# Spacing the weight loads of a two-layer recurrent transformer kernel in its plan, and moving the zeros of its value tiles

## The chip, the cores and the metric

The kernel runs on one core of a Trainium2 chip. The core has five engines that work side by side and wait for each other through semaphores: the PE (TensorE, matrix products), ScalarE (ACT in the profile), VectorE (DVE), GpSimd (POOL) and SyncE (SP, which here only starts transfers). GpSimd starts transfers too. The metric is the device time of one execution in microseconds (us).

## The reference

Two layers are applied twice, with the same weights each time. Layer A is an attention that goes through the sequence in 64 segments of 32 rows; eight memory rows are put in front of each segment, and the memory of the next segment is the output of this one. So the segments follow each other strictly. Layer B is a gated feed-forward. The reference, cut:

```python
def A(x, mem0, Wq, Wk, Wv, Wo, seg_len):          # x: 1 x 2048 x 512, 32 heads of 128, memory 8 rows
    mem, outs = mem0, []
    for s in range(n_seg):                        # 64 segments
        h = concatenate([mem, xs], axis=1)        # 8 + 32 rows
        q, k, v = h @ Wq, h @ Wk, h @ Wv          # per head
        p = softmax(where(mask, q @ k.T * scale, -1e9))
        o = (p @ v) @ Wo
        mem = o[:, :M, :]                         # goes on into the next segment
        outs.append(o[:, M:, :])
    return concatenate(outs, axis=1)

def B(x, w_gate, w_up, w_down):                   # 512 -> 1792 -> 512
    return (sigmoid(x @ w_gate) * (x @ w_up)) @ w_down

x = x + A(layernorm(x));  x = x + B(layernorm(x))
x = x + A(layernorm(x));  x = x + B(layernorm(x))
```

## The kernel before

The kernel runs the two passes of layer A interleaved: step t does segment t of the first pass and segment t - 6 of the second, so most matmuls have 80 columns (twice 40 rows). The attention weights stay in memory on the core. The feed-forward weights do not: each block of 128 rows loads all of them again, in pieces of 256 KB, into rings of three tiles each for `wg`, `wu` and `wd`.

The program is not written down in its final order. Each operation is added to a planner as a task, with the engines that may do it, an assumed duration in ns, what it reads and writes, and for a transfer the bytes `nb` and a latency `lat`. The planner then walks through time with a simple picture of the chip, and takes on each free engine the ready task that comes first in a stored sequence. The order in which the tasks start in this picture is the order in which the instructions stand in the program, engine by engine. So the assumed numbers change no instruction's real duration; they change which instruction stands where, and what a load waits for.

```python
class Planner:
    LAT = {"PE": 205.0, "DVE": 110.0, "ACT": 128.0, "POOL": 40.0, "SP": 4000.0}
    BUS, LEAD, TAIL, BIG, ROOM, POOL0 = 345.0, 2000.0, 1900.0, 200000, 300.0, 2000.0
    ...
    def forward(self):
        ...
        # GpSimd does not take a big load while the transfer queue is too far ahead
        if e == "POOL" and T[q[1]].nb >= self.BIG and bus > now + self.LEAD + self.ROOM:
            aside.append(q)
            heapq.heappush(events, (bus - self.LEAD - self.ROOM, 1, 0))
            continue
        ...
        if tk.nb:                                  # when a transfer lands in the plan
            bus = max(bus, now + self.LEAD) + tk.nb / self.BUS
            done = bus + self.TAIL
```

A feed-forward weight load, and the matmuls that need it (`B` is called `ffn`):

```python
pl.add("POOL", 760, lambda wg=wg, fs=fs: nc.gpsimd.dma_start(out=wg[:], in_=self.wgv[:, :, fs]),
       r=[("wo", self.H - 1)], w=[gk] + bt, lat=4600.0, nb=2 * self.DC * P * P * 2)      # 262144 bytes
...                                                # the same for wu and wd
GB = pl.buf(self.bank, "bg")                       # PSUM bank; at most 3 of kind "bg", 3 of kind "v"
pl.add("PE", 2 * DC * mm_ns(n), mm, r=[xk, gk, uk], w=[GB])        # L1034: gate and up
...
pl.add("PE", 2 * mm_ns(512), dm, r=[hk, dk], w=[DB])               # L1058: down
```

The spacing in the plan is carried over to the chip: each big load gets a wait on the last PE task that had ended, in the plan, when the load started.

```python
for tk in order:
    if tk.on == "POOL" and tk.nb >= self.pl.BIG:
        k = bisect.bisect_right(ends, tk.start + 1.0)
        if k:
            pace[tk.idx] = pes[k - 1].idx
...
    if tk.idx in pace:
        self.tc.add_manual_dep(nc.cur_bb.bb.instructions[-1], seen[pace[tk.idx]], self.SYNC, ...)
```

GpSimd also clears tiles at the start, among them rows 32 to 63 of the three value tiles, which must be zero because the product with the probabilities runs over 104 rows and only 80 of them hold values:

```python
for k, t_ in enumerate(self.vsb):                  # 3 tiles, [128, 2, 1024] bf16
    pl.add("POOL", 1860, lambda t_=t_: nc.gpsimd.memset(t_[32:64], 0.0), w=[...])
```

Other lines that the profile names: L834 query and key products, L848 scores, L862 to L879 softmax, L891 transposes of the probabilities, L914 product with the values, L932 product with Wo, L682 and L759 value products (in full tiles and in strips of 32 rows), L651 and L1002 transposes, L641 the power of the layer norm, L1150 matmuls on a zeroed tile `hot` that only keep the PE busy, L1158 copies on ScalarE, L1160 copies on VectorE.

Of the kernel before, what the change touches and what calls it, by code (L numbers as in the profile page):

```python
# [20 lines left out]
P = 128  # L21
MEM = 8
SEG = 32
L = MEM + SEG
# [29 lines left out]
;AiJ8O<e#G00LqO81Dpg?#XRnVk#=3t=h#IvY(+`&AcaUnw28X=}w4PEU`lamQ$OIpo&~BNLA*v)8_<LH_4?mqJB9BPoKci*ww~Xp)w?&I~Z~HBw)uo$QQx-;`OBtJB6xFkfX<JRX)Vp<pwi9-$>Wq  # L54
_|(bG)+LpP5u9QR&=8D1Ynn6`50CKLwAk)5&^1p?M5ud)kVw93aBRaf&q*h3JD;4Ll!hLLRQPlXLpBL((>{FtthZ7-6|on*(`sH;)5N{G{S1Q90H4$Ds(Z|lR0?u{tEC`hGou%Gd$027BUNC18E{L7
&F)C#zgM=c{I#A@-&_cC)EA7@W+gT`4MdX5Z<e~;XBiD0b6uuRW+zpR5($+!E$PDMb#05@4J<$Tgbufr7=j;14{hrW2XG!0l#o*PC@hFM#?tGT6r9A)HO<OTl13v9w~w#YRv#=MeGw>(WPyyKB1!Cc
Kh4|7Igw&V<X;!vy&=LHaWFD+p%tHofD6TKnCr|$0|AFqvW@S36%&P<g+xP2B_-vSh>c$a21QjVdvj4tl9}JapL&LM5}J5*o7wnh^Q!>iVtS2`P40J?4<hBBT!d|vv(!65R|43k?j2ySJjDalB!M5q
0+48MexK=31cV1eCa9G4=FYg0$8pi>H?<rNeHU|4WBR@wD1Gs|PFGshWAv`I7x-d~N80)*!h<rk^pgB$#xYA8^3<cts1d0#zHflM9<Kn7(59`#h`o$$C3RD8h@e)twdz3~B2ztI-Zl=|>k0(jtN&EZ
M+6(<F}aBH*s>|C;8a&rtX~-hVfXD<h6X~?EY^Zz6gi0r<U9i(>VzMAJE*Se^dOX0rgm~|E!=Xx9r_TrDzwc0+!EsrL~)Soi;Oi;HUFoX=*13GNv&ZMt+nOX`)*VNh$X0KjWg3pTl4!=JTaVM>8>HL
847pxUL$IK>({v}PsAcpnD@J-@IuLIgQ_IF-p$l|+Y>W~r)<#N&!w#H{kF|?*-F)dKD!wIm9RA>Xq1LJ2Wok$$C~rlfyiSKy6@0|B)T>H1NJUFd;RLgL9*+RWXJx?QqOd)T>|2m?ALU71CBZm<cDwJ  # L60
ofeVYFF39i25%~7b6dl-Szt!`b-re7-B~{crk)vUJfH3kryVB*(7RtNQcI^zOIYp)7{`a^=;Ws?VKJ)*;5|5eFn<A8j@jc(VHL0+6_~v%wV&XqjHFI1AMwQBZ_@YmyTCt@Qzj;730DaCS=SbvOAy#R
b*Sqhur|1y$EZAJ1;bN)$+7$=8C~Lo*;Hrsm6OARmhEF(!s4()P-}CtMCgoM?F;6)-20FEkTpVQ?bo7ItMHTYNO09xJ8>TRYqO*|GTUQCd45=t;TTVkp2mNk?%z5;D%B{z#Ebw;WE>3bKD}~M8i*5L
$e=1i%D_S#Xj_x8+IE7dP}suAIjN}(q`q-QX}`+C;;ka@YIYS}2&7Qm<f>$oR=*)*I`|4m=LBs&(Q!LT1;Q>IcRD}S@&NS($)uVXEtMjw&vna78_S7Mlec%u<sO~)mngVW7>T6h$iUEYqnP|puo0fT
r`TMWmfzTh<G(BWf)#O<t!5y74sH_M&Z=4btV4*QNiV4<6V&W{e4I*MRws<_x%O(Y$MOrVEeoVyG3@QId`iX^5p6WM8c$3kg{SO5{l)C7p}yI}4CaD%!l71<san+GQCJk+p}VL~bP8uJkGY0kBT5vj
R1-ykT=4ub<1V=InVbNwl6!S8td%+Mz~(^8*x_;GPz>g2$XSqPPbev-o^hs!?7@QMWhY0y`$$F&9ixb+y?zfPat4Fi!9lU1Pg8vI&j;+LEM7n1u5gq)5A1Ko>q-PF|9fW{quMQz<qKqqK}c6+c+Fjd
F2Og)Y9!)bPmT?k!nyf?G)Xd5=K!N;M>3lVNE}6P7cnNl4OcV-lb#H=@=tK=cxvWNb6Kzv_sM|QR*voi!Zn`=jVh#r4%=)b)LoY?p68N_b^*GwHypnifULn;3GbuLC`r8UsPf=vI`9TA8B`u7X6;#N
!m;8u{taW8B=ZYuhxB9*O)W#qWE!7AhkB;}qi!mEvlh~K9<WKouf7f7L{WqYu}gBY?M2l)tmM{7Nu9QfNYq2fype%X^IJqHYC#4qRVe@~VAmgkHN0m|{HV|^C7s-nFqYkrf5W*?th9LSf%-sleh6@c
h^ng>)=Ywn0;fa0nILORo|102uL^+jVT+d!dfe14p)J)dlR1OmXGPfL-y36CdZ?|rcwsM+BZtm`w8J3fxRJ_+4s6&Uno5Bi_*n7}#H?RWtb4Zi&|Rm*Zz2TNh&lO#7UGXjAdPbxNHJ|g_4H9xi8*?+
MVBMu<!Xv~TZTq;8n*wB%JxEkrMB;<8}+JQA_z}uHS0xv7nP9H@k*%6*aeBVs5=pHO`T#wtNbE}<|rvhkGwM4E;)G7MYl*s$M|Wb`VP#Re6BgJ2e|qxS57L9bw0omcy&;%c|qJ{(zEm8exBk>6kxD6
nxVA2ia}k;GP?4Q>rk`340>lGd_YNLHVqb}3U`2d_S9|fmyu5SUIT|O7ON>xv0wK}^_@-tG>TrZhfljsqoh53@*TnfA+x8TWApG@0BvWO*~un;YD}WAVB`%Ocf`pScOENCOw%nLPstoRq_M;BvJb5(  # L70
9>G{3K!TD={~^49yc*?mqNgGc5Y9`P58_BH7xzKfFPZ`Ggp&M|jB=z<d!Mk7Cu<-nf0j1JK3){GSBO4_Z3Mk$J5xc&swnx5Kk-kQoc7)9dxA>^2fUiVDTTmJUDH?8OUBger)cDkijH?|-1he<?wF<H
Kk8n|8|izgJ<_+Vk)Z%3oi>GZ`YrtS_<S>K*lk;jOpIxLM&`FEhlm;kTVot3q|rBV<2zngWEolEcY`CX0@8r^=@owQoZaOwbLKKB5WYQ9ATLkYUM6T<RE#Alz-kX8EZD3nbuenjKH^OPbNyU7wVF39
J|$N?ZCflXfOCh2K(_Em93YBI;A{RAe?$e%i<!x3qM)(DsREc-Dh@|;RaZz{Ll-kv@m+)8ts@E#1fh>1JG<CwJGMH~u9ZKP6{u*%L%13ENMvluV`@wIuxV8YVb)3nInI0dgPfb`)M|>%G*b`M+Eyyj
jqV1HH2csu+-gLZN!CnTWAkDUlaM(`w_&JSZYO|vzbuZQ*3PLKI)0ga%QxJf?^bvE1F+>TX${_k_>1jSMGlLjj>YIweuT`hQ?^&irkU=_GGO$DDI{>cW;6n|9j!RtGy%M~@}&-R?w${HkEp`&f?|dq
hRtUsFPVbG8-up0*v|ZA*EkVFY50Mj6?9y)4JpMkyC%&ExAc7!4gc+R=<99a<n4o-&ZXVwa+QJY{b7j7VJQE>0Y8piWd%VS48RwJid2BAY66-+%Wl?{`zc4poCF9pm`~fP$UOlA=c$<fqq-V>@sE|3
N2~z048Fb9GPveh@ym=U;`2r6)y6OIo@9rAM5%*f0;`aD^F_98-YHoGz4`oih2?qv)`GZ>QO83Z7HvL5ku>dZiIYj=NO}ck>~z#R9*jNmjj|h>R>*3!dO|Qd*G>CP;It>Jo_T;GC~pf_h0K-$@9NV(
Yc?%zR57pmwZF@3z4b@VylrfJgY8hUsQH8ZBkkZq&^W*i-SfqeRO5NrAvXkh&g(F!yM}aT2C%-OF2xzXzKSs;={nZ6_yf?1CIP>lDI%J_4+iG0e0Y*9L@sdrmoxK;-^O}^j{s;#33QVj&{6E{)c`(a
0m2$#FN9>Go~9^QTaLqSiZ*BMF#UuZ2jV|#zFyP{6ZIfV|6w=QBC6Nk74ljq;^E9%i7<mDgdu`P)*G%KFS9NhI@jYCWV;!fE?F(PTURqbC5r+G%lI3Ds5u3dhs(YNO(hU!r9zfn7Z)&Np35;9CW#Ix
Nhdqy(G=`Uwwx<tm0DUwS`j-vH=40;MIKh=C8++MOn+jHr&b!1HaeP8q27%Wwvr!fjWty(7P_w*Y6ZhSmNk;>)&>Nr!2_ToBVK24<Z_uWphcS+bz5U394$%Sb@B4EDXBD{qki}0)M{yRH@}u6M7wCh
TTLh0(<NnDqs~#M`T}!1V!b5Vi?3Al_Ch9h%WvHFl_Ao6&#>CZDmjK2s%yAB2NwlkWT+U;W1=eC6#(P~y9k=oudM_^fL$0(g`o5?7cc_|^bL$Ni5kPR`SogUK{9>o>|3B-G~crq=gC+1PhzO&^)-{>  # L80
AL$G9*1n#@HI$4bYS$00_^%r;MjbaTk-h>#gMKLjOUX`o3_g#oChX&Mw<l~T@d!0uh}(6DI2uvbBW=pzFI3g&ba;I~t)tmpWEzCr(#xgmTsW-^Oo5#^<_1&{TT7T2QNzvm6V$+U@+y@<nOxQT#A`bl
v<3QcoFW=8$eG<>u4h!T-3^@RtBOQT)}%Fziq+(Qq$L4e#j=$6<dutOS#HJ%P^#PTtR|8!<V)}Pl-QDt?*W{n5$R=VpV+TvJeCQYJD<qzU(>7v)vrFI77jTNEfw*5ALJ-_Z=Ti)zNKgUt<IE${bO}G
w;Kv*X;Az|q}iV$*Gu0E8r@nVZSTH@=Cu~^bLM!ob@#C}hZZJcy|;K{M-pLkbu{JGj38i<Y+EgeXAdPS)ROjlBTsjCLtPyY>l;W_Bk^l=kb57Wrb7)<M6UoP#Hw+O;~5WhgWQh1jhI8)H>EE^+dMlS
T&F|)OSR$mljIZ;MD6PzZ}g#Hmjy2WDn~)PS#<58+n5$O(f`Q{T=&<uktF>c125T$r3R{Yz{&6T)6?34T!dJPHBXrRZ0h3ziUXEIhQLc*K!oX!T1^MLiAyj%(BCi(dI-zZH=Oj!#y~!NV_U29M2ORV
tZlhP{4K&Raoz=c@<+IwLussb<<<Bg%iTl7nQ^c0X_4!idtroxhvg#5pI@#@V%NrQzNEKXW(G^o8rmhaJDf<O)grV8;HQc)>a**4gyovjts79IdHVf$rTIOhxO_628kzExc=mNb>(eaxkAqT{%q@WT
&^LG~>5B9CpIc%i2RDTv@#vLD<sW$8Q;mKd`+|ho2Aw|u7Ukl4-_uzwx`vttzyXqg=WwrBv(>ujNbY}T()ENYunSuycC*ux7u%sgaf7C@CBZ%^59jC$dHhoATFhjt<w!w27%c;FzxY433X}3Q5Z<kk
YXbesw?eHY*<T_mm~tr4dO-JGxanG#IDrzX^+0!gx3To=#8IePThSLmcWNTP4(MG`ZP%VLbs?6|@7#`AGE{5$Z9hfBFS}sANw3rFcpc5%^~wYPPLMh?qpUV!mBu#Td|w{WuaJG@B?j!CHdy!Jmwu);
TNLHt9>X6tJas%iKrk29$cyO#!h=#Hd9iat`7Na_Z(STpxyV{V_S9`jgN6z$tyny<r)pg#W2^sKyr`Mqcl%MVviZO#sOTg_$YKq89Vhom_uSb-Tx)2L9YL+-Ubu^Nn|2#8SVJ222?@Kb#g7Dm<_Cor
KVp{AEoBrUjr8jLcvA5@ALY(btw?6uJ*_AZCTY-2-$tjBhz~tBt?seBkxRT7?~8a7C!IUN0qH+i4BwLC23<-*eaD*0mi$?9WBqnV&P9Q--E`HXEy!Yl&8bp&qU=`<A%IRRD0ba^z9?a>oN1L}?WA)!
7-KVRbbefi>p4@}UBO1Yqus=;UjG6j(x6G&|CzVaHNa`%HWk8;@&5WxfC@+9<2^)5#A15g>t<&mgo=+Pjp=W=>VcqbdY(;wDr@7EC}GC+NfM(%_u?|o%+kmlhCBn$i)p{c7^at+@!sXP6J#s{9iPJj  # L90
MgKCyGw>8$fZt0=)}?C=&bsG+4M1f^-<2Tkz1hmA0xCM_g!rZTEv~N5-*zW7bOP=TmOdV$x+KTx5NdiIF37M{G_XYac(TTF`MZ=Y=t-O5biad#+<Y+$g1UO+yj)}wKzDK0+fVXuK1_IAZXtQxI&#;9
W7L95)KW9tUhMr4bQ7)QuUa!LK-m5hNf1mZKsaB-=7BNJi-3drDH+F)Svbe1&jM4^u{jEf^7gz**sPb|66Rp>9(D&S?254s3fK9IHFiw2SxM5FX%UF=w-*-Ke>oS}KfGxd{kl0Tf-HH@`LfUxO>F84
2)_IJ*DHqc=ejOeCYGY+Q<2!$2@{kncf(O+y#=9&$D6Zwr=ilP1N6{m1f4J{okK`@NT63iS?;ExD==8w^+QAa=n3NINnNQlKS&j8Xuwir7<riQXN1b+f~#5ja8wNF6R$+@m%zMRspuN}(y|tiitgPh
;Jshe#)AhGpsyv?yc~8^1vSu2D#EF2dKNV7$9sAf2hKG16LpN;cxK{D$SQlP1oSRP38kp7<mwvAN`M{Hr=2DRZ3;ZGWkEo;E;M{Ek>OOd13XrSGlGEoJRQMJQ-wHvn{j)=51=H7X8w216q`!ZSSZ?G
V?PDT78H>^jfiNrKBmDNc!-#o!FvKR8KQ9lE8@l$83KubJGBDBCMB-toOh+18!)gcY=Rkosl?9<Sf<z!|L1eOP=+6M_2EQ-Al*#(#!~g<z$cNsTm|FrhIa7jlZ>dRn7~Opa;SNWpW^Su19WZbT$lw9
UYRELKfc~K6Ib_z^nq1DzH|dDjU^zZO%TEe$k#r=eu9&dlyX>06;-PE4Wan7VDMWZ)4-T-RdnOoVwL53uHNZhp0m3xR6xe9NBBIPYn8S;wF|Vbl~ySVGfjWoh+O)1&c2{hFzw)?9|2WzYFD+q!W|)b
t-X^r&S;-LiC?kP$jXbR%|f*xawf#`^R4plRetezPKbIe4CHB|tC)%&2fXa+d!3y?eXhfoQ7Hn&TDhTAwrWVMgLjEzVcK5zVXOW!gimknFt%M{7O*aEU`T<1Bc0cm#swk3faVuQu32FVvW6y(vGeC(
`r6uA87|)l%@cYO^cp4MKd{;mm6xzxul7M71fKj6_=}m*9k`n5el)6dXRSszBHj?3{A5RHjXWh<OfQm^68hnLIK)wmX`^OTGIVmuYGd2ituQWg_*#^aje<wsHPI<>&&`wLf!d}FVp-Xv)MoC`WGk9r
# [90 lines left out]
class Planner:  # L189
# [79 lines left out]
    def forward(self):  # L269
        T = self.tasks  # L270
# [6 lines left out]
        bus = 0.0  # L277
# [36 lines left out]
        while left:  # L314
# [6 lines left out]
            for e in free:  # L321
# [45 lines left out]
                if tk.nb:  # L367
                    bus = max(bus, now + self.LEAD) + tk.nb / self.BUS
                    done = bus + self.TAIL
# [852 lines left out]
```

## Time and profile before

| | |
|---|---|
| time, median of 3 runs | 1833.38 us (1831.83 to 1837.33) |
| span of the profiled run | 1841.1 us |
| mean granted clock of the PE | 0.997 |
| feed-forward weight loads (wg, wu, wd) | 220 of each listed, 256 KB each |
| median from issue to landing | 5.0 us (wg), 5.0 us (wu), 5.2 us (wd) |
| transfers started by GpSimd | 183.09 MB, 33.9% of the 16 engines' time |
| transfers started by SyncE | 82.20 MB, 15.7% |

The profiled run is a little longer than the timed ones, so its numbers are read as shares and differences. Engine rows give busy time, share of the span and number of instructions. A matmul row's mean duration (198 ns for 80 columns) is longer than the interval between two of them, because they overlap; the time that one really takes is the interval from its start to the next one's. In the list of waits, each row names the engine, the line, what the wait ended on, the total in us, the number of waits and the longest. The line of a landing DMA names the tile and the tensor it came from.

### The profile page before, as it was taken

How to read it: one execution, taken by the hardware profiler on the slowest of the kernel's cores; microseconds unless marked ns; L12 is line 12 of the kernel's file. 1: busy time of each engine (PE TensorE's matmuls, PEld its weight loads, DVE VectorE, ACT ScalarE, POOL GpSimd, SP SyncE). 2: the span in 40 equal slices, each digit the busy share in tenths (PEclk: the TensorE clock that was granted, in tenths of full speed). 3: DMA queues.
4: the chain of work that ended last, by engine and by line, in shares of the span. 5: the costliest groups of instructions: out<-in, count | busy, mean ns of one | idle time of the engine just before them, and what ended most of it. 6: DMA issues, size and time to landing. Idle time of an engine off the chain costs nothing.

```text
span 1841.1 us, 92142 instructions
## 1 busy us (share of the span) xinstructions
PE 1794.3 (97%) x40036; PEld 1528.2 (83%) x40036; DVE 1148.3 (62%) x3911; ACT 1183.4 (64%) x2992; POOL 580.4 (32%) x836
## 2 busy tenths in 40 slices
PE   9999999999999999999999999999999999999998
PEld 4677888888788888889888898988888897889886
DVE  4466556676565667566665566576655764566665
ACT  5666656666665667666665766566765765666564
POOL 6413032422333241323324241333324231333432
PEclk9999999999999999999999999999999999999999
DMA  9824254634555463555536453555546354554543
GB/s 316 295 71 139 59 148 117 178 109 130 153 156 157 116 185 86 160 152 160 157 110 187 135 161 100 165 154 145 166 134 181 106 158 114 151 157 120 173 129 101
DMA packets 137112, 271.19 MB, mean 147 GB/s; under 512 B 32650, under 2 KB 69138, under 8 KB 136706
## 3 DMA queue, kind: packets, MB, share of 16 engines
q0 software_dynamic: 56608, 183.09, 33.9%
q1 hardware_dynamic: 80098, 82.20, 15.7%
q8 instruction: 314, 5.14, 1.2%
q14 instruction: 92, 0.75, 0.1%
HBM read 220.93 MB, written 26.21 MB: 134 GB/s over the span
## 4 chain that ended last, share of the span: by engine, by line
PE 76%; DMA 6%; issue 6%; DVE 5%; POOL 3%; ACT 3%; SPq 0%; POOLq 0%; ACTq 0%; DVEq 0%
PE bank L834 28%; PE bank L932 13%; PE bank L682 8%; PE bank L1034 8%; PE bank L759 6%; PE bank L1058 4%; PE bank L914 3%; PE bank L848 3%; DMA wd<-in_B_w_down_dram 2%; DMA wg<-in_B_w_gate_dram 2%; DMA wu<-in_B_w_up_dram 2%; PE bank L891 2%; DVE st L862 1%; POOL wu L1027 1%; POOL wg L1026 1%
## 5 line engine op out<-in xcount | busy, mean ns | idle before, releaser
L834 PE MATMUL bank<-hT,wq_sb 128*128 128x80 bf16 (+1 forms) x8960 | 621.4, 198 | 0.5 <-issue 0.5
L834 PE MATMUL bank<-hT,wk_sb 128*128 128x80 bf16 (+1 forms) x8960 | 621.1, 198 | 0.5 <-issue 0.3
L1158 ACT CAST qku<-bank 128x480 bf16<-128x480 f32 (+3 forms) x770 | 386.7, 512 | 233.3 <-PE bank L834 137.1
L834 PEld LDWEIGHTS <-wq_sb 128*128 128x128 bf16 x8960 | 454.1, 99 | 32.8 <-issue 22.5
L834 PEld LDWEIGHTS <-wk_sb 128*128 128x128 bf16 x8960 | 450.7, 99 | 0.9 <-issue 0.8
L862 DVE TENSOR_TENSOR st<-bank,cst 40x240 f32<-40x240 f32 (+3 forms) x768 | 276.8, 367 | 239.2 <-PE bank L848 224.5
L932 PE MATMUL bank<-otsb,wo_sb 128*128 128x80 bf16 (+1 forms) x8960 | 364.7, 198 | 3.8 <-ACT otsb L1158 2.4
L932 PEld LDWEIGHTS <-wo_sb 128*128 128x128 bf16 x8960 | 339.1, 99 | 22.9 <-issue 7.2
L1026 POOL DMA_DIRECT2D wg<-in_B_w_gate_dram x217 | 163.6, 754 | 266.4 <-PE bank L1034 119.4
L1027 POOL DMA_DIRECT2D wu<-in_B_w_up_dram x217 | 163.9, 756 | 262.4 <-PE bank L1034 110.4
L1158 ACT CAST otsb<-bank 128x480 bf16<-128x480 f32 (+3 forms) x420 | 198.0, 483 | 69.2 <-PE bank L914 54.3
L1052 POOL DMA_DIRECT2D wd<-in_B_w_down_dram x217 | 153.3, 708 | 223.9 <-PE bank L1058 131.8
L1158 ACT COPY ptsb<-bank 40x240 bf16<-40x240 bf16 (+3 forms) x563 | 179.4, 321 | 48.3 <-PE bank L891 38.0
L872 ACT ACTIVATE st<-st 80x240 f32<-80x240 f32 (+3 forms) x420 | 159.0, 381 | 53.4 <-DVE st L869 50.6
L641 POOL TENSOR_TENSOR small<-small,cst 128x1 f32<-128x1 f32 (+1 forms) x80 | 45.3, 568 | 440.4 <-DVE small L640 435.1
L1034 PE MATMUL bank<-xnT,wg 128*128 128x128 bf16 (+2 forms) x1784 | 172.8, 219 | 6.8 <-DMA wg<-in_B_w_gate_dram 6.2
L1034 PE MATMUL bank<-xnT,wu 128*128 128x128 bf16 (+2 forms) x1784 | 172.2, 219 | 3.8 <-DMA wu<-in_B_w_up_dram 3.5
L874 DVE TENSOR_REDUCE small<-st 80x6 f32<-80x240 f32 (+3 forms) x420 | 151.3, 362 | 35.7 <-ACT st L872 32.8
L848 PE MATMUL bank<-qku 128*128 128x80 bf16 (+1 forms) x2240 | 162.4, 198 | 2.1 <-issue 1.7
L879 DVE TENSOR_TENSOR pb<-st,small 80x240 bf16<-80x240 f32 (+3 forms) x420 | 153.7, 369 | 4.5
L869 DVE TENSOR_TENSOR st<-st,small 80x240 f32<-80x240 f32 (+3 forms) x420 | 153.8, 367 | 3.0
L867 DVE TENSOR_REDUCE small<-st 80x6 f32<-80x240 f32 (+3 forms) x420 | 151.3, 362 | 4.4
(97 smaller groups left out, 2326.9 us busy)
## 6 DMA issues: line engine op xcount, KB each, us to landing
wg<-in_B_w_gate_dram POOLq DMA_DIRECT2D x220, 256.0 KB, 5.0
wu<-in_B_w_up_dram POOLq DMA_DIRECT2D x220, 256.0 KB, 5.0
wd<-in_B_w_down_dram POOLq DMA_DIRECT2D x220, 256.0 KB, 5.2
vsb<-scr SPq DMA_DIRECT2D x476, 48.0 KB
vsb<-sst SPq DMA_DIRECT2D x480, 32.0 KB
scr<-vst SPq DMA_DIRECT2D x120, 96.0 KB
wq_sb<-in_A_Wq_dram SPq DMA_DIRECT2D x10, 384.0 KB
wo_sb<-in_A_Wo_dram SPq DMA_DIRECT2D x10, 384.0 KB
```

The costliest lines, as they stand in the source:

```text
L834: nc.tensor.matmul(o_ap, lhsT=W[:, c, h * P:(h + 1) * P], rhs=mv(c), start=(c == 0), stop=(c == DC - 1))
L848: nc.tensor.matmul(s_all(SB)[:, w0 + i, :], lhsT=fview(qku[:, i, 0, 0:1], [(1, P)]), rhs=qku[:, i, 1, 0:ncol], start=True, stop=True)
L862: pl.add("DVE", dve_ns(n, True), lambda gsz=gsz, hs=hs, st=st, SB=SB, pj_=pj_, npj_=npj_, mk=mk, idx=idx: nc.vector.tensor_tensor(out=st[p ...
L869: pl.add("DVE", dve_ns(n), lambda gsz=gsz, hs=hs, st=st, mx=mx: nc.vector.tensor_tensor(out=st[pr, hs], in0=st[pr, hs], in1=mx[pr, hs].uns ...
L872: pl.add("ACT", act_ns(n), lambda hs=hs, st=st: nc.scalar.activation(out=st[pr, hs], in_=st[pr, hs], func=ACTF.Exp, scale=self.scale), r=s ...
L879: nc.vector.tensor_tensor(out=pb[pr, hs, 0:L], in0=st[pr, hs], in1=rs[pr, 0:gsz].unsqueeze(2).to_broadcast([npart, gsz, L]), op=ALU.mult)
L932: nc.tensor.matmul(WB[:, c * ncol:(c + 1) * ncol], lhsT=self.wo[:, h, c * P:(c + 1) * P], rhs=otsb[:, hl, 0:ncol], start=(h == 0 and c == ...
L1026: pl.add("POOL", 760, lambda wg=wg, fs=fs: nc.gpsimd.dma_start(out=wg[:], in_=self.wgv[:, :, fs]), r=[("wo", self.H - 1)], w=[gk] + bt, la ...
L1027: pl.add("POOL", 760, lambda wu=wu, fs=fs: nc.gpsimd.dma_start(out=wu[:], in_=self.wuv[:, :, fs]), r=[("wo", self.H - 1)], w=[uk] + bt, la ...
L1034: nc.tensor.matmul(gu[:, 2 * i + k, 0:n], lhsT=W[:, c, i * P:(i + 1) * P], rhs=xnT[:, c, rw], start=(c == 0), stop=(c == DC - 1))
L1052: pl.add("POOL", 760, lambda wd=wd, ip=ip: nc.gpsimd.dma_start(out=wd[:], in_=self.wdv[:, 2 * ip:2 * ip + 2, :]), w=[dk] + (["boot"] if se ...
L1158: nc.scalar.copy(out=dst, in_=src)
```

## The change

The change touches the plan in three places. First, a weight load now counts 370,000 bytes in place of 262,144 in the plan's transfer queue, since it shares the transfer engines with the value tiles; it may be issued only when the queue is free (room of 1 ns in place of 300), and it never counts as landed before its own latency, now 5200 ns after its issue has ended. The limit above which a load is spaced goes from 200,000 to 300,000 bytes. The real transfers keep their size. Second, the zeros of the value tiles are written by copies from the zeroed tile `hot` on ScalarE or VectorE, whichever the plan picks, and no longer by GpSimd. Third, the last 32 rows of the last block take their PSUM banks from the other kind, so that they do not compete with the 96 rows before them. The stored sequence of tasks is replaced by a new one that belongs to this plan. What the program computes stays the same.

```diff
 SEQUENCE = r"""
-;AiJ8O<e#G00LqO81Dpg?#XRnVk#=3t=h#IvY(+`&AcaUnw28X=}w4PEU`lamQ$OIpo&~BNLA*v)8_<LH_4?mqJB9BPoKci*ww~Xp)w?&I~Z~HBw)uo$QQx-;`OBtJB6xFkfX<JRX)Vp<pwi9-$>Wq
...                                      (the whole stored sequence is replaced)
-    BUS, LEAD, TAIL, BIG, ROOM, POOL0 = 345.0, 2000.0, 1900.0, 200000, 300.0, 2000.0
+    BUS, LEAD, TAIL, BIG, ROOM, POOL0 = 345.0, 2000.0, 1900.0, 300000, 1.0, 2000.0
...
-                        heapq.heappush(events, (bus - self.LEAD - self.ROOM, 1, 0))
+                        heapq.heappush(events, (bus - self.LEAD - self.ROOM + 0.5, 1, 0))
...
-                    done = bus + self.TAIL
+                    done = max(bus + self.TAIL, end + tk.lat)
...
         for k, t_ in enumerate(self.vsb):
-            pl.add("POOL", 1860, lambda t_=t_: nc.gpsimd.memset(t_[32:64], 0.0),
+            pl.add(("ACT", "DVE"), {"ACT": 1760.0, "DVE": 2200.0}, lambda t_=t_: (t_[32:64], fview(self.hot[32:64, 0:1], [(0, 2), (0, 1024)])),
...                                      (wg; the same for wu, wd and the last block's weights)
-                pl.add("POOL", 760, lambda wg=wg, fs=fs: nc.gpsimd.dma_start(...), r=[...], w=[gk] + bt, lat=4600.0, nb=2 * self.DC * P * P * 2)
+                pl.add("POOL", 760, lambda wg=wg, fs=fs: nc.gpsimd.dma_start(...), r=[...], w=[gk] + bt, lat=5200.0, nb=370000)
...
-            GB = pl.buf(self.bank, "bg")
+            GB = pl.buf(self.bank, "v" if more else "bg")
...
-        DB = pl.buf(self.bank, "bg")
+        DB = pl.buf(self.bank, "v" if more else "bg")
```

## The prediction

> **What bounds the kernel now.** I read the page's engine row first, then the waits of the PE, then the windows and the timeline around the longest of those waits.
>
> ```profile
> PE 1794.3 (97%) x40036; PEld 1528.2 (83%) x40036; DVE 1148.3 (62%) x3911; ACT 1183.4 (64%) x2992; POOL 580.4 (32%) x836
> ```
>
> The PE is the bound: every other engine has a third of the span free. It sits idle for 1841.1 - 1794.3 = 46.8 us; that, plus pauses too short to show as idle, is all that a better order can win, because the matmuls stay the same. How much is in short pauses: adding up the usual start-to-start interval of every matmul (in this trace 36 ns for 80 columns, 25 for 40, 56 for 128, 216 for 512; the strips on L759 1.84 us for 32) gives about 1738 us, so about 100 us of the span is not matmul work, half of it in pauses that the busy figure hides.
>
> Second view, what the PE waited for:
>
> ```profile
> engine line waited for: us in total, times, longest us
> PE bank L1058 <- DMA wd<-in_B_w_down_dram: 10.9, 8, 2.8
> PE bank L1034 <- DMA wg<-in_B_w_gate_dram: 6.2, 9, 2.5
> PE bank L1034 <- DMA wu<-in_B_w_up_dram: 3.5, 6, 1.1
> PE bank L1002 <- ACT oxT L1158: 2.6, 6, 0.5
> PE bank L651 <- DVE xn L642: 2.6, 3, 1.7
> PE bank L914 <- ACT ptsb L1158: 2.5, 11, 0.3
> PE bank L932 <- ACT otsb L1158: 2.4, 7, 0.6
> ```
>
> The three largest are all feed-forward weights that had not landed. With 0.4 us for the last block's weights (a line further down) they make 10.9 + 6.2 + 3.5 + 0.4 = 21.0 us in 24 waits, almost half of the idle time. No other cause is over 2.6 us.
>
> Third view, the timeline of GpSimd before the longest of these waits (start, duration, line, count):
>
> ```profile
> 462.07 1.49 POOL L1026 DMA_DIRECT2D wg<-in_B_w_gate_dram  x2
> 463.54 0.75 POOL L1027 DMA_DIRECT2D wu<-in_B_w_up_dram  x1
> 464.28 1.44 POOL L1052 DMA_DIRECT2D wd<-in_B_w_down_dram  x2
> 466.87 0.71 POOL L1052 DMA_DIRECT2D wd<-in_B_w_down_dram  x1 [1.14 <-PE bank L1058]
> ```
>
> and the PE at its end:
>
> ```profile
> 472.29 0.59 PE L1058 MATMUL bank<-wd,hff 128*128 128x512 bf16 x2 [2.84 <-DMA wd<-in_B_w_down_dram]
> ```
>
> Five loads leave in 3.7 us, as fast as GpSimd can issue them (0.75 us each). The second wd of that burst leaves at about 465.0 and the PE gets it at 472.29, over 7 us later. Windows over the same place (PE, PEld, DVE, ACT, POOL busy, PE clock, DMA share, GB/s):
>
> ```profile
> 462.00:469.00 7.00, 7.00 (x154) 6.24 (x150) 5.97 (x23) 4.97 (x14) 5.80 (x9) 1.00 0.98 284
> 469.00:473.00 4.00, 1.16 (x23) 0.82 (x20) 0.39 (x2) 0.20 (x1) 0.12 (x1) 1.00 0.78 244
> 473.00:477.00 4.00, 4.00 (x59) 3.87 (x55) 0.50 (x2) 1.11 (x4) 1.14 (x2) 0.57 0.38 101
> ```
>
> Two things are to be seen. The transfer engines are full (0.98) while the burst lasts, though over the whole span their mean is half of that: the loads wait for each other. And after the stop the PE clock is 0.57 for 4 us: a second cost of one wait. The stop at 1521 shows the same, with a clock of 0.59 in the 4 us from 1524.
>
> I then sorted the 672 weight loads of the trace by how many others left in the 4 us before. Median time from issue to landing: 3.5 us with none, 4.0 with one, 4.6 with two, 5.1 with three, 5.9 with four, 6.2 with five; longest 8.3 us. The plan before counts on 2000 + 760 + 1900 = 4660 ns for a load that finds the queue empty. That is right for two neighbours and 1.3 to 1.6 us short for four or five, and 255 of the 672 have four or five.
>
> **What the Trainium skill says.** "DMA: Bandwidth & Descriptors", section Issuing engines are not separate DMA queues: transfers from all engines run on the same 16 engines and interleave. The trace agrees: the 0.98 above includes SyncE's value-tile transfers. The same page, Anatomy of one DMA, gives about 2.0 us plus bytes over 436e3; for 262,144 bytes that is an estimate of 2.6 us. No load here lands under 3.1 us, and 3.5 alone is usual, so the measurement decides; the plan's old figure leaned the same optimistic way. "TensorE: Matmul & The Clock Gate", What's actually happening: the PE's clock is halved after an idle window of about 3.4 us. The trace agrees in kind: two stops of some 3 us were followed by 0.57 and 0.59. "Perfetto Trace Analysis", Identifying the Most-Contended Engine, warns that matmul busy time does not tell the distance to the limit; that is why I added up intervals above.
>
> **The change part by part.**
>
> (a) Spacing. In the plan a load now takes 370,000 / 345 = 1072 ns of the queue instead of 262,144 / 345 = 760, may be only 1 ns ahead of a free queue instead of 300, and never counts as landed before 760 + 5200 = 5960 ns. The recorded PE instruction that releases each load makes this real on the chip. To see it I walked both programs in the order in which they stand and summed the intervals above from the instruction that releases a load to the first matmul that needs it. Before: 11 of 672 loads have under 5.0 us of PE work to hide in, 104 under 6.0, 184 under 7.0. After: none, 4 and 73. Loads with four or more others released within the preceding 4 us of PE work: 298 before, 45 after; the usual number is now three, which lands in 5.1 us at the median and 7.0 at worst. Adding 0.3 us (an allowance of mine for release and issue), the median landing overruns the lead for 66 loads before and for none after. So of 21.0 us I expect 1.5 to stay: -19.5 us.
>
> (b) Clock. Without the two stops of some 3 us the slow stretches go: 4 x (1 - 0.57) + 4 x (1 - 0.59) = 3.4 us. -3.4 us.
>
> (c) Zeros of the value tiles. Three memsets of 1.80 us leave GpSimd (5.4 us); in the new order ScalarE copies two and VectorE one from a zeroed tile, as their first work, before any input has landed. Before, a power instruction of the layer norm stood behind one of those memsets (6.70 to 8.53) and the PE then waited 1.67 us for xn at 11.79. In the new order the short memsets come first and the powers in a row behind them, so part of the gain is handed back. After 12 us the start is bound by weights (DMA share 0.94 and 0.89 in the first two slices of 46 us) with the PE at 42.2 and 45.1 of 46. I count -1 us.
>
> (d) Order. Feeding the weights at a wider spacing leaves less freedom elsewhere. Measured in PE work as above, the tenth percentile from a query/key group to its scores falls from 1.08 to 0.97 us, the median of the softmax chain (scores to the transposes of its result) from 5.47 to 5.32. The PE's waits on ScalarE and VectorE results come to about 9 us after the first 130 us; with leads 3 to 10% shorter, and short pauses beside them that do not show as waits, I add a quarter of that: +2.5 us.
>
> (e) Bank kind. Bank limits in the feed-forward of the last 32 rows are those of the value kind now, so it need not queue behind the 96-row part. The end from 1794 loses 5.3 us of 47, but in the new order more filler matmuls stand in the last stretch (45 units of 128 columns against 27 in the PE's last 12 us of work), a sign that the gaps are not gone: 0.
>
> Sum: -19.5 - 3.4 - 1 + 2.5 = -21.4 us; 1833.4 - 21.4 = 1812 us.
>
> **The rivals.** First, the waits only move: wider spacing pushes loads into stretches where the value-tile transfers run, or in front of the PE later. For it: SyncE moves 82 MB on the same engines. Against it: the leads grew together with the spacing, and the mean use of the engines is about half. It would return 8 to 12 us: 1822. Second, the stops take up slack that other chains need; without them, copies and softmax come under pressure and the hidden short pauses grow. For it: the shorter leads in (d); ScalarE and VectorE are busy 64% and 62%, so they have room on average but not at every place. It would cost another 6 to 10 us: 1820. Third, the new order is better beyond the transfers, in the 50 us of hidden pauses: 1800. Nothing in the leads speaks for that.
>
> **Range and chances.** 1812 us, with 1803 to 1824 for 8 times in 10: the upper end is half of the transfer gain lost, the lower end all of it and some of the short pauses. Faster by over 2% needs 1797 or less, that is 36 us of some 100 us that are not matmul work: chance 0.04. Slower by over 2% would need a new stop of the size of the whole idle time: 0.01. Within 2%: 0.95.
>
> **What would show it.** (a) Waits of the PE on the three weight tensors together under 4 us, longest landing near 7 us instead of 8.3. (b) No window with a clock near 0.6 after the start. (c) No memset of the value tiles on GpSimd, and the first value matmul (L682) before 12.7 us. (d) Waits of the PE on ScalarE and VectorE 2 to 3 us higher. I am wrong if the transfer waits stay over 8 us, or if they go and the span does not follow.

## The result and the profile after

| | before | after |
|---|---|---|
| time, median of 4 runs | 1832.94 us (1831.83 to 1837.33) | 1809.57 us (1809.46 to 1810.16) |
| ratio, after to before | | 0.9869 (95%: 0.9852 to 0.9886) |
| span of the profiled run | 1841.1 us | 1807.9 us |
| idle time of the PE in it | 46.8 us | 26.2 us |
| longest landing of wg, wu, wd | 8.3, 7.9, 8.1 us | 6.0, 6.3, 6.0 us |

The change saves 23.4 us in this batch of runs. The kernel before was timed again beside the experiments and came to medians of 1836.60, 1836.49 and 1835.65 us (7, 7 and 15 runs); the changed kernel was not timed again, so its gain is known to some 4 us, and where a later run is set against it below, the two come from different batches. The profiled run before took 1842.9 us, 10 us more than its median, so the two traces differ by 33 us; this has to be kept in mind when waits from a trace are set against times.

The engine row of the page after:

```profile
PE 1781.7 (99%) x40039; PEld 1524.2 (84%) x40039; DVE 1152.3 (64%) x3919; ACT 1189.6 (66%) x2987; POOL 580.5 (32%) x838
```

The work of the other engines is the same to within 7 us; the PE is busy for 12.6 us less with the same matmuls. Some 8 us of this are the parts of pauses that count as busy (worked out below). Some 5 us are the clock: the trace before has three stretches of 3.4 us at half clock, two after the stops that the prediction names and one at 12.6 us, and the trace after has none. The waits of the PE after (engine, line, what the wait ended on: total in us, number, longest):

```profile
engine line waited for: us in total, times, longest us
PE bank L1002 <- ACT oxT L1158: 4.6, 10, 0.5
PE bank L932 <- ACT otsb L1158: 4.4, 10, 0.7
PE bank L651 <- DVE xn L642: 3.5, 2, 2.9
PE bank L848 <- ACT qku L1158: 1.5, 5, 0.5
PE bank L914 <- ACT ptsb L1158: 1.3, 7, 0.2
```

The three weight rows, 20.6 us before, are gone; no weight load is in the list at all. What leads now are results of ScalarE, and one wait of 2.9 us at the start. The timeline of GpSimd in the same block of the sequence as the burst shown before:

```profile
457.31 0.70 POOL L1052 DMA_DIRECT2D wd<-in_B_w_down_dram  x1 [0.66 <-PE bank L932]
458.52 0.78 POOL L1026 DMA_DIRECT2D wg<-in_B_w_gate_dram  x1 [0.50 <-PE bank L891]
459.70 0.71 POOL L1052 DMA_DIRECT2D wd<-in_B_w_down_dram  x1 [0.41 <-PE bank L914]
461.13 0.77 POOL L1026 DMA_DIRECT2D wg<-in_B_w_gate_dram  x1 [0.72 <-PE bank L932]
461.90 0.75 POOL L1027 DMA_DIRECT2D wu<-in_B_w_up_dram  x1
```

and the windows there (PE, PEld, DVE, ACT, POOL busy, PE clock, DMA share, GB/s):

```profile
460.00:464.00 4.00, 4.00 (x81) 3.11 (x82) 1.07 (x3) 1.68 (x7) 2.76 (x5) 1.00 0.81 245
464.00:468.00 4.00, 4.00 (x100) 3.23 (x90) 0.96 (x2) 2.32 (x5) 2.07 (x3) 1.00 0.88 270
468.00:472.00 4.00, 4.00 (x117) 4.00 (x114) 3.67 (x13) 2.66 (x6) 0.57 (x1) 1.00 0.46 122
```

The loads leave about every 1.2 us in place of 0.75, most of them released by a PE instruction of their own, and these five land in 3.9 to 4.3 us. The PE is busy in all of the 12 us, at full clock.

Two tables from the traces serve as measures below. First, the 672 weight loads by the number of others that left in the 4 us before, with the median landing:

| others | 0 | 1 | 2 | 3 | 4 | 5 |
|---|---|---|---|---|---|---|
| before, loads | 71 | 75 | 110 | 161 | 171 | 84 |
| before, landing us | 3.50 | 4.03 | 4.60 | 5.06 | 5.94 | 6.22 |
| after, loads | 69 | 69 | 138 | 364 | 32 | 0 |
| after, landing us | 3.47 | 3.85 | 4.23 | 4.48 | 4.88 | |

Second, by how much the start-to-start intervals of the matmuls exceed their usual length, counted where one does so by over 150 ns: 68.6 us in 166 pauses before, 40.1 us in 111 after. So the pauses fell by 28.5 us, where the idle figure shows 20.6. The excesses of 5 to 150 ns, added up in the same way, hardly changed: 48 us before, 47 after.

### The profile page after: what moved, and what is told of

Read it like the earlier page. It is cut to its first block, busy times and chain, and to the rows that moved or that the text cites. A ratio compares the mean times of both kernels' runs of the same rounds, so it can differ in the third digit from the quotient of the medians.

```text
span 1807.9 us, 92108 instructions
## 1 busy us (share of the span) xinstructions
PE 1781.7 (99%) x40039; PEld 1524.2 (84%) x40039; DVE 1152.3 (64%) x3919; ACT 1189.6 (66%) x2987; POOL 580.5 (32%) x838
## 3 DMA queue, kind: packets, MB, share of 16 engines
q8 instruction: 314, 5.14, 1.2%
## 4 chain that ended last, share of the span: by engine, by line
PE 89%; DVE 4%; ACT 3%; DMA 1%; issue 1%; SPq 0%; POOL 0%; ACTq 0%; DVEq 0%; POOLq 0%
PE bank L834 31%; PE bank L932 16%; PE bank L1034 11%; PE bank L682 8%; PE bank L759 7%; PE bank L1058 5%; PE bank L914 4%; PE bank L848 4%; PE bank L891 2%; DVE st L862 1%; ACT ptsb L1158 1%; PE bank L651 1%; ACT qku L1158 1%; DVE small L867 1%; DVE small L874 1%
```

## The experiments

All are timed beside the kernel before. Theory 1: what counts is the PE work that stands between the release of a load and its use, and it is the order that makes it. Theory 2: what counts is that the loads do not leave close together. Theory 3: the order gains in pauses of other origin. "Lead" below is that PE work.

**The old order under the new spacing, and the new order under the old spacing.** Both plans have the same tasks in the same numbering, so the stored sequences can be exchanged. Both runs keep the new zeros and bank kinds. The expectations count leads anew and come to slightly other numbers than the prediction (115 loads under 6.0 us before, where it has 104).

```diff
 # e1: after.py
-SEQUENCE = <new>
+SEQUENCE = <the one of before>
 # e2: after.py
-    ... = 345.0, 2000.0, 1900.0, 300000, 1.0, 2000.0        lat=5200.0, nb=370000
+    ... = 345.0, 2000.0, 1900.0, 200000, 300.0, 2000.0      lat=4600.0, nb=2 * self.DC * P * P * 2
-                    done = max(bus + self.TAIL, end + tk.lat)
+                    done = bus + self.TAIL
```

> The changed kernel with the stored sequence of before: the new spacing, zeros and banks alone. Walked as in the prediction, 78 of 672 weight loads have under 6.0 us of PE work to hide in (115 before, 4 after), and 110 leave with four or more others in 4 us (289 before, 29 after). Theory 1 (what counts is the PE work between a load's release and its use, and the sequence made that): about half of the gain, 1819 to 1828 us, waits on the three weight tensors 6 to 14 us. Theory 2 (what counts is that loads no longer leave in bursts): nearly all of the gain, 1809 to 1815 us, waits under 4 us.

> The changed kernel with the old spacing in the plan (262,144 bytes, 4600 ns, room 300, no floor on the landing), new stored sequence kept. 9 of 672 loads have under 6.0 us of PE work, but 189 leave with four or more others in 4 us. Theory 1: 1809 to 1815 us, waits on the weights under 4 us. Theory 2: waits of 8 us or more, 1818 to 1828 us.

The old sequence under the new spacing took 1855.41 us, ratio 1.0107 (1.0089 to 1.0126): slower than before. Neither theory had that. The lines of its list of PE waits that matter:

```profile
PE bank L932 <- ACT otsb L1158: 6.7, 20, 0.7
PE bank L914 <- ACT ptsb L1158: 4.8, 18, 0.6
PE bank L891 <- DVE pb L879: 4.4, 13, 0.6
PE bank L914 <- DVE ptsb L1160: 3.9, 11, 0.5
PE bank L834 <- DVE hT L945: 3.8, 9, 0.8
PE bank L1034 <- DMA wg<-in_B_w_gate_dram: 1.2, 2, 0.8
```

The spacing did its part: waits on the three weight tensors are 1.6 us in all. Theory 2 had said under 4 us and theory 1 6 to 14, so for these waits theory 2 was right: 78 loads still have leads under 6.0 us, but the longest landing is 6.9 us in place of 8.3. (The PE's other waits also give each load more time; the two are not separated.) The time went elsewhere. After the first 130 us the PE waits 29.7 us for ScalarE and VectorE, against 8.5 us before, and the planner puts in more matmuls that only keep the PE busy (L1150: 141 in place of 94; after the 15th us they take 26.6 us of the PE in place of 17.8). The trace is 11 us longer than that of before; these matmuls make 9 us of it, and the waits, 21 us more here and 19 us less on weights, 2. The likely reason is that the feed-forward matmuls, now held back in the plan, no longer fill the places where the attention chain needs something to lie beside it; no run shows this alone.

The new sequence under the old spacing took 1815.62 us (1812.96 to 1815.95), ratio 0.9887 (0.9865 to 0.9909), with no weight tensor's wait over 0.7 us. That is theory 1, 0.6 us above its range. In its trace 172 loads leave with four or more others, 28 of them with five, which take 6.0 us to land at the median, but their leads are long enough. So the sequence carries most of the gain, and the spacing the last 3 to 6 us (3 by the ratios, 6 by the times; the ratio intervals of this run and of the changed kernel overlap, the run times do not). What is lost there is not a wait on feed-forward weights. The trace has 3.6 us of pauses of the PE with no releaser, against 0.7 in the changed kernel, one stretch of 3.4 us at half clock just after the longest of them (1.42 us, up to 166.04), and the 0.7 us for a weight of the last block. What these pauses are is shown below, with the runs without recorded waits.

**Half loads in the old order.** This takes the suspected cost away and leaves every queue's order as it was.

```diff
-nc.gpsimd.dma_start(out=wg[:], in_=self.wgv[:, :, fs])
+nc.gpsimd.dma_start(out=wg[:, 0:m], in_=self.wgv[:, 0:m, fs])     # m = 2 of 4 after the first ring turn; wu, wd alike
```

> The kernel before, order untouched on every engine, but each weight load after the first turn of the rings moves only half of its bytes (the other half of the tile keeps old values, so the output is another). Median landing should fall to about 3.5 to 4.3 us. If the weight waits are what the change removed: 1810 to 1817 us, waits on the three weight tensors under 3 us. If the new order gained elsewhere (theory 3: short pauses of other origin): no better than 1824 us.

It took 1808.35 us (1807.93 to 1808.83), ratio 0.9851 (0.9834 to 0.9869). Its output is another one, since half of each tile is stale. Lines of the wait list of this run, without its first, and its median landings:

```profile
PE bank L1002 <- ACT oxT L1158: 2.6, 6, 0.5
PE bank L914 <- ACT ptsb L1158: 2.5, 11, 0.3
PE bank L932 <- ACT otsb L1158: 2.4, 7, 0.6
PE bank L891 <- DVE pb L879: 1.5, 5, 0.4
PE bank L1034 <- DMA wg<-in_B_w_gate_dram: 1.2, 1, 1.2
```

```profile
wu<-in_B_w_up_dram POOLq DMA_DIRECT2D x214, 128.0 KB, 3.2
wg<-in_B_w_gate_dram POOLq DMA_DIRECT2D x214, 128.0 KB, 3.2
wd<-in_B_w_down_dram POOLq DMA_DIRECT2D x214, 128.0 KB, 2.9
```

The four rows on ScalarE and VectorE are those of before, to the tenth; the waits on weights fall from 21.0 to 1.7 us, and the pauses of the PE without a releaser from 2.9 to 0.4. So the full loads cost the old order 1836.60 - 1808.35 = 28 us, nearly all of it through late weights and the clock after them, and the old order had nothing else of size that the new one improves: theory 3 falls. The new order, at 1809.57, is within 1.2 us of the old one with its weights in time.

**Half loads in the new order.** The same edit on the changed kernel.

> The changed kernel with half the bytes in each weight load after the first turn of the rings (another output, as in the half loads of the kernel before). If the changed order leaves nothing of the transfer cost: 1807.5 to 1810 us, the same as the changed kernel, and no better than the 1808.35 us of the old order with half loads. If crowded transfers still cost it something beside the visible waits: 1800 to 1806 us.

1809.22 us (1808.46 to 1809.53), ratio 0.9848 (0.9827 to 0.9868). Halving the bytes brings nothing any more; the transfers are off the path altogether.

**No recorded wait.** The same order on each engine, but a load leaves as soon as its tile is free; the third run keeps the recorded waits only near the end of the plan.

```diff
-                if tk.idx in pace:
+                if tk.idx in pace and False:                                            # e4 (after.py), e10 (before.py)
+                if tk.idx in pace and tk.start > pes[-1].start - 200000.0:              # e11 (after.py)
```

> The changed kernel with the same order on every engine, but without the recorded wait of each weight load on a PE instruction: a load leaves as soon as its ring tile is free. All loads then have 6.0 us or more to hide in, but 146 leave with four or more others. Theory 1: the same time, 1807 to 1812 us, weight waits near 0. Theory 2 (the prediction's wording that the recorded wait makes the spacing real and so the gain): bursts return, 1815 us or more, waits of 4 us or more.

> The kernel before without the recorded waits of the weight loads. In its order a load's release is mostly set by the ring tile coming free: without the recorded waits 107 loads have under 6.0 us of PE work (115 with them). Theory 1: no help, 1832 to 1845 us, waits on the three weight tensors 12 us or more. If the recorded waits released the loads too late and that was the cause: under 1825 us.

> The changed kernel with recorded waits only for weight loads that start in the last 200 us of the plan. Without any recorded wait the time was 1815.2 us; against the changed kernel some 1.5 us were lost by the 140th us and some 4 us in the last 40. If that is all they do: 1810 to 1812 us. If they matter all along: 1813 us or more.

On the changed kernel: 1815.18 us (1814.86 to 1815.84), ratio 0.9889 (0.9872 to 0.9906). Theory 2 had the right time, but not its reason: no weight tensor is in the list of waits. The place is found by setting equal events of the two traces side by side: 1.7 us are lost by the 25th us, then the distance stays within 2 us up to the 1770th, and the last 37 us cost 4 more. The loss at the start is not a wait on a load: it is a stretch of 3.4 us at half clock from 9.0, which delays the first value matmul from 11.88 to 13.55. At the end the last block's weights go into twelve free tiles, which no ring holds back. Eleven of them leave between 1774.5 and 1782.7, and they land late:

```profile
wv_sb<-in_B_w_up_dram POOLq DMA_DIRECT2D x4, 256.0 KB, 6.6
wv_sb<-in_B_w_down_dram POOLq DMA_DIRECT2D x4, 256.0 KB, 6.1
wv_sb<-in_B_w_gate_dram POOLq DMA_DIRECT2D x4, 256.0 KB, 6.7
```

The same 10 us without recorded waits, and then in the changed kernel:

```profile
1780.00:1790.00 10.00, 7.87 (x166) 6.83 (x166) 6.18 (x24) 4.98 (x17) 2.65 (x4) 0.83 0.72 214
```

```profile
1780.00:1790.00 10.00, 9.11 (x194) 7.24 (x189) 9.06 (x37) 6.27 (x23) 5.66 (x8) 1.00 0.62 171
```

The PE loses time and its clock falls to 0.83. Its two pauses there have no releaser in the profile:

```profile
1780.68 0.19 PE L848 MATMUL bank<-qku 128*128 128x40 bf16 x1 [1.66 <-issue]
1786.90 0.20 PE L1034 MATMUL bank<-xnT,wu 128*128 128x96 bf16 x1 [1.29 <-issue]
```

They are waits of the PE for its own program, which comes over the same transfer engines: the page of every run lists 314 transfers of 5.14 MB in a queue of kind `instruction`, 16 KB each.

```profile
q8 instruction: 314, 5.14, 1.2%
```

The trace lists 80,373 instructions of the PE, so one such transfer holds about 256. Counted over all 14 traces, the PE has 45 pauses without a releaser. All 45 end at the same place in a piece of 256, to within three instructions, and 1.2 to 2.1 us after the end of such a transfer. The traces that have the new order with spaced loads hold 0.3 to 1.2 us of these pauses, the three that have it with crowded loads 2.8 to 4.3 (4.3 here). So what crowding costs the new order is, but for 0.7 us, not late weights but late instructions, and the half clock that followed two of these pauses.

With recorded waits only near the end, the landings of the last block's weights are 4.1, 4.3 and 3.9 us and the time is 1811.58 us (1809.73 to 1812.84), ratio 0.9860 (0.9838 to 0.9882). On the kernel before, taking the waits away changes nothing: 1835.65 us, ratio 0.9996 (0.9984 to 1.0009), with 17.8 us of weight waits.

Do the recorded waits space the loads in the body of the run? In the changed kernel 32 loads leave with four or more others, without recorded waits 132, with them only near the end 124, and in the kernel before 255. So order and rings (a load leaves when the third use before it is done) halve the crowding, and the recorded waits take away most of the rest. But with them only near the end the time is 2 us longer than with all of them, so in the body the extra spacing is worth little; the leads are 6.0 us or more there without it. At the end it is worth 4.

**Later releases.** The same order on PE, ScalarE and VectorE, each load released by the PE instruction that ends 1 or 2 us later in the plan.

```diff
-                k = bisect.bisect_right(ends, tk.start + 1.0)
+                k = bisect.bisect_right(ends, tk.start + 1.0 + 2000.0)     # 1000.0 in e12; loads placed behind that instruction
```

> The changed kernel, the same order on PE, ScalarE and VectorE, but each weight load is released by the PE instruction that ends 2 us later in the plan. The shortest leads fall: 28 loads under 4.5 us and 79 under 5.0 us of PE work (0 and 0 in the changed kernel), while the number of loads that leave close together stays (34 with four or more others, 29 in the changed kernel). Theory 1 (lead): adding 0.3 us to the median landing, 37 loads fall short by 12 us together; 1816 to 1828 us, waits on the three weight tensors 6 to 15 us. Theory 2 (bursts alone): 1809 to 1811 us.

> As the release 2 us later, which took 1847 us, but 1 us later: 4 loads under 5.0 us of PE work, 30 under 5.5. Lead against the median landing plus 0.3 us gives a shortfall of 0.5 us in all (12.5 us at 2 us later, where 18 us of waits on weights came and 37 us of time). Theory 1: 1810 to 1816 us, waits on weights under 4 us. If a delay costs in proportion, whatever the lead: about 1828 us.

2 us later: 1847.02 us (1843.49 to 1848.97), ratio 1.0058 (1.0040 to 1.0076). 1 us later: 1819.86 us (1819.05 to 1821.84), ratio 0.9908 (0.9886 to 0.9929). The loads are no closer together than in the changed kernel, so bursts alone are refuted: shorter leads bring the waits back. But both cost more than the leads said (1816 to 1828 and 1810 to 1816 us). In the first, the weights make 18.1 us of the waits (2.7 us in the second). The line numbers of this kernel's helpers are six higher:

```profile
PE bank L1034 <- DMA wg<-in_B_w_gate_dram: 9.4, 15, 1.3
PE bank L651 <- DVE xn L642: 8.2, 10, 2.0
PE bank L1034 <- DMA wu<-in_B_w_up_dram: 6.4, 9, 1.2
PE bank L1002 <- ACT oxT L1164: 4.6, 10, 0.5
PE bank L932 <- ACT otsb L1164: 4.2, 10, 0.7
PE bank L848 <- ACT qku L1164: 2.9, 7, 0.9
PE bank L1058 <- DMA wd<-in_B_w_down_dram: 2.3, 4, 0.8
```

The second row was 3.5 us in the changed kernel and is 6.5 in the run with 1 us. GpSimd also takes the power of the layer norm, and in its program the power stands behind loads that now wait longer for their release. One such place in the run with 1 us, on GpSimd and then VectorE:

```profile
788.40 0.71 POOL L1052 DMA_DIRECT2D wd<-in_B_w_down_dram  x1
789.55 0.72 POOL L1052 DMA_DIRECT2D wd<-in_B_w_down_dram  x1 [0.45 <-DVE st L869]
790.29 0.57 POOL L641 TENSOR_TENSOR small<-small,cst 128x1 f32<-128x1 f32 x1
```

```profile
788.59 0.14 DVE L640 TENSOR_SCALAR small<-small 128x1 f32<-128x1 f32 x1
790.89 0.41 DVE L642 TENSOR_SCALAR xn<-xs,small 128x512 bf16<-128x512 bf16 x1 [1.10 <-POOL small L641]
```

The input of the power was ready at 788.73; it started at 790.29, behind two loads. The PE waited 0.7 us for xn there. The rest of the 37 us, beyond the visible waits, was not traced further.

**The zeros and the start.** Three runs on the first 12 us.

```diff
 # e6: zeros on GpSimd again
-pl.add(("ACT", "DVE"), {"ACT": 1760.0, "DVE": 2200.0}, lambda t_=t_: (t_[32:64], fview(self.hot[32:64, 0:1], ...)),
+pl.add("POOL", 1860, lambda t_=t_: nc.gpsimd.memset(t_[32:64], 0.0),
 # e7: all three on ScalarE
+pl.add(("ACT",), {"ACT": 1760.0}, ...
 # e8: after the plan, clears of pb, ptsb, qku and the third zero (as a memset) behind the second power on GpSimd
+order = [tk for tk in order[:places[-1] + 1] if tk not in down] + down + order[places[-1] + 1:]
```

> The changed kernel with the zeros of the value tiles as memsets on GpSimd again (1.80 us each). The lead of every weight load is the same as in the changed kernel. If moving the zeros mattered as the prediction had it: 1 us slower, 1810.2 to 1812 us, with the first value matmul later than 11.88 us. If the start is bound by something else: the same within 0.5 us.

> The changed kernel with all three zero copies on ScalarE, so none on VectorE. In the changed kernel the mask selection on GpSimd took 1.34 us beside the VectorE copy (0.29 before). If that copy holds GpSimd up: 0.3 us again, the powers about 1 us earlier, the first value matmul near 11 us and the time up to 1 us shorter. If not: no difference at the start.

> The changed kernel, on GpSimd the clears of pb, ptsb and qku moved behind the second power of the layer norm, and the third zero copy made a memset on GpSimd behind them too, so VectorE is free. The PE waited 2.95 us for xn at 9.00. Expected at the start: xn ready 2 to 3 us earlier, first value matmul at 9 to 10 us. If nothing else binds the start: 1807 to 1808 us. If the weights that arrive in the first 90 us bind it (transfer engines full in the first 46 us): the time within 0.5 us of the changed kernel's.

Zeros on GpSimd: 1815.45 us (1814.61 to 1817.11), ratio 0.9890 (0.9875 to 0.9904). In the new order the three memsets stand first, 5.28 us in one piece, the first power comes at 11.76 in place of 7.34 and the first value matmul at 15.76 in place of 11.88; 4.0 us are lost by the first attention step and 5.8 by the end. All on ScalarE: the first value matmul comes at 10.83, a microsecond sooner, and it brings nothing: 1810.59 us (1808.63 to 1813.74), ratio 0.9864 (0.9846 to 0.9881). The PE then meets the value weights themselves:

```profile
13.29 1.02 PE L682 MATMUL bank<-wv_sb,xvf 128*128 128x512 bf16 x4 [0.33 <-DMA wv_sb<-in_A_Wv_dram]
```

Powers ahead of the clears: the first transposes of the layer norm at 7.08 in place of 9.00, but the third power now stands behind the clears, the PE waits 2.72 us for it at 15.26, and the time is 1813.68 us (1812.45 to 1815.04), ratio 0.9881 (0.9864 to 0.9899). None of the three took the time that was expected of it. A start up to 1 us earlier is not worth anything here; a start 4 us later costs 6.

No version beat the changed kernel by its median; the only faster ones moved half of the weights.

## Why the prediction was right

The time foretold was 1812 us (1803 to 1824); it came to 1809.57. The main cause is shown, but that the sum came so close is in part luck: (a) was too small and (d) too large, and (b) was read from a run slower than most. Its parts:

- **(a) Spacing, -19.5 us.** Right in the mechanism, too small in size, and with one step wrong. All weight waits went, where 1.5 us were to stay, and the longest landing fell from 8.3 to 6.3 us. With its weights in time the old order gains 28 us against the kernel before of its own batch, and 24.6 against the median of 1832.94; (a) and (b) together gave 22.9. The list of waits counts only the idle part of a pause, and the end of the matmul before it covers the rest. Wrong was that the gain hangs on the recorded PE instruction: it does make the spacing real (32 crowded loads with it, 132 without), but without any recorded wait the kernel before is the same and the changed one loses 5.6 us, 4 of them at the end. Nor is PE work between release and first use a measure that holds by itself: it told the releases 1 and 2 us later from the changed kernel, but e1, with 78 loads under 6.0 us of lead, has 1.6 us of weight waits where 6 to 14 were expected from it. A load is late when its landing exceeds its lead; the spacing shortens the one, the order lengthens the other, and the changed kernel does both.
- **(b) Clock, -3.4 us.** Right for the two traces: no stop on a weight is left, and no window after the start is near 0.6. But 3.4 us was read from a run at 0.997. Of the 29 runs of the kernel before in the later batches, nine have a mean clock of 1.000, thirteen 0.999, four 0.998 and three 0.997; the nine took 1832.92 us at the median, still 23 us more than the changed kernel. So in most runs this term is under 2 us, and the gain is there without it.
- **(c) Zeros, -1 us.** The first value matmul came at 11.88 in place of 12.72, as if the start had gained 0.8 us. This is not shown: the old order with half loads, whose start is that of the kernel before, has it at 11.97, and the changed kernel without recorded waits at 13.55. Inside the new order the move is worth 5.9 us, because that order puts the memsets first; against the kernel before that is not the right measure.
- **(d) Order, +2.5 us.** The waits on ScalarE and VectorE after 130 us rose from 8.5 to 11.8 us. The cost in time is about 1 us (half loads in both orders: 1809.22 against 1808.35), and up to 1 us more if (c) helped the first of these; the two stem from different batches. So the term was too large.
- **(e) Bank kind, 0.** No run undoes it alone. Left open.
- **The rivals.** "The waits only move" did not come true for the changed kernel, but it is just what e1 shows when the spacing comes without its sequence: 19 us of weight waits gone, 21 us of other waits back. "Slack that other chains need" is the same thing. "A better order beyond the transfers" is refuted by the half loads, and the short pauses that it was to draw on stayed at 47 of 48 us.

## What to carry to other kernels

If a trace blames late transfers, halve their bytes with every order left alone: the time that comes out shows about how much those transfers cost, and here the change got within 1.2 us of it. A new cost in the planner did not pay by itself here; it removed the wait it was meant for and handed the time to the next chain, until the sequence was replaced with one made for it. Here either long leads or spaced loads were enough to have the weights in time, but crowded loads also held up the PE's own program. Before adding a release to a load, see what holds it already (a ring tile, the queue before it), and what stands behind it on the issuing engine.

## What was not expected of the hardware

- The spread of run times went with the clock. The kernel before ran from 1831.38 to 1835.71 us in the nine later runs with a mean clock of 1.000 and from 1837.98 to 1843.09 in the three at 0.997.
- The PE can run short of its own program: up to 1.66 us at a time, and 4.3 us in all in one trace. In the new order with half loads it does not happen at all.
- At half the bytes the neighbours nearly stop mattering: in the new order the median landing is 2.64 us with no other load in 4 us and 2.74 with three, where full loads take 3.47 and 4.48.
- A VectorE copy can hold up GpSimd. The mask selection on GpSimd took 1.34 us in the changed kernel, where VectorE copies zeros from 1.00 to 2.22, and 0.29 us with that copy on ScalarE:

```profile
1.03 1.34 POOL masks.py:199 TENSOR_SCALAR_AFFINE_SELECT cst<-cst 128x128 bf16<-128x128 bf16 x1
```

```profile
1.03 0.29 POOL masks.py:199 TENSOR_SCALAR_AFFINE_SELECT cst<-cst 128x128 bf16<-128x128 bf16 x1
```

The Trainium skill, "SBUF — State Buffer", section Who interferes with whom, says that a VectorE copy in a two-port mode and GpSimd block each other for a whole instruction, whichever starts first. The two lines agree, with 1.05 us of delay beside a copy of 1.22 us; that this copy ran in such a mode is not shown by the trace.
